# First block of a clustered attention + gated FFN kernel as a software pipeline, with one PSUM tile per logits side

## Chip, cores, metric

One Trainium2 chip, one core of it. The metric is the device time of one execution in microseconds (us), median of several runs. Ratios are computed as the mean time of one kernel's fast runs over the mean of the other kernel's fast runs of the same rounds, so a ratio is not quite the quotient of the medians quoted beside it.

In the text: PE is the matmul engine, DVE the vector engine, ACT the activation engine, POOL the general one. "Issuing queue" is the SyncE queue, from which 146 of the 150 DMAs of the kernel before are issued, in the order of the program. The "granted clock" is the share of full speed at which the profile shows PE's clock: 1.00 is full, 0.50 half. DVE's `avs` step adds the value sums to a finished av result and so frees its bank.

## The reference

Attention in which a key counts for a query only where both fall to the same of 16 clusters, then a gated FFN. Batch 4, 8 heads, sequence 768, head size 64; FFN from 512 to 1536 and back, on 3072 tokens.

```python
q_assign = argmax(einsum('bhsd,hcd->bhsc', q_n, c_n))      # k_assign alike
mask = q_assign[:, :, :, None] == k_assign[:, :, None, :]
scores = where(mask, scale * q @ k.T, -1e9)
attn = softmax(scores); x = attn @ v                       # heads side by side: [3072, 512]
out = (sigmoid(x @ w_gate) * (x @ w_val)) @ w_out
```

## The kernel before

Each batch is done in two blocks (half of the queries each): eight blocks. A block is 24 steps: 4 pairs of heads times 6 chunks of keys. A step makes scores (2 matmuls), one exp on ACT, and, one step later, 6 matmuls with the values ("av"). The FFN of the block before is mixed into it, some 5 matmuls a step; after block 8 its FFN runs alone (the tail).

Before scores can be made, a pair must be prepared: split into high and low halves of fp16 (`hl`), transposed into `T`, multiplied with the centroids (logits), turned into one-hot rows, and these transposed into 16 further rows of `T`. Scores contract over 80 rows of `T`, 64 of data and 16 of one-hot.

```python
    def logits(b, side, pr):                     # one PSUM tile for both sides
        if side == 1:
            CL[b, pr] = fp_.tile([128, 2, 256], FP, name="f")
        ...
    def prep_pe(pr):                             # batch 0, pair by pair, on PE
        for side in (1, 0):
            hl = split(b, side, pr)              # two DVE instructions
            pt = scp.tile([128, 2, 1024], HP, name="sc")
            ... # 12 transposes, copy to T (DVE for side 1, ACT for side 0)
        for side in (1, 0):
            logits(b, side, pr); onehot(...)
        for side in (1, 0):
            ... # 12 transposes of 80 rows, copy of 16 rows into T
    def att(b, qb):                              # 24 steps
        for pr in range(NPR):
            for j in range(NCH):
                ... # scores into sc (2 buffers), exp into es
                yield
                if pend is not None: av_part(*pend)   # at j == 5: avs = av + sv on DVE,
                ...                                   # which frees the only av bank
                yield
    def ffn(b, qb, tail=False):
        for fc in range(NFC):
            for i, w in enumerate((wg, wv)):
                ...
                for dc in range(NDC):
                    nc.tensor.matmul(out=gv[i][:, 0:QB], ...)
                    yield
            g = gp_.tile([128, QB], FP, name="g")
            nc.scalar.activation(g, gv[0][:, 0:QB], AF.Tanh, scale=0.5)
            nc.vector.scalar_tensor_tensor(hT[:, fc, :], g, 1.0, gv[1][:, 0:QB], ALU.add, ALU.mult)
        ...
    def plan(b):                                 # preparation of batch b within batch b-1
        for pr in range(NPR):
            a = 6 + 8 * pr
            at(max(a - 9, 0), load_pair, b, pr)
            at(a, prep_a, b, pr)                 # splits, DMA transpose
            at(a + 8, prep_b, b, 1, pr)          # logits, onehot
            at(a + 9, prep_b, b, 0, pr)
        ...
        at(40, prep_oh, b, 1); at(41, prep_oh, b, 0)   # one-hot: DMA transpose, 8 row DMAs
```

The softmax here doesn't subtract the row's maximum and nothing guards it: scores larger than these inputs give would overflow.

## Time and profile before

| | before |
|---|---|
| time, median of 3 runs | 414.63 us (413.35 to 415.19) |
| span in the profile | 411.4 us |
| first exp starts | 20.99 us |
| block 1, first exp to first exp of block 2 | 58.85 us |
| blocks 2 to 8, same measure (the last to the last exp) | 44.46, 42.42, 45.40, 43.02, 46.65, 38.46, 35.99 us |

Block lengths here and below are counted from the start of every 24th exp in the timeline. Blocks 7 and 8 prepare nothing.

Busy time by stretch, cut where the transpose of a block's output is issued. The columns are stretch, its length, then busy us (and instructions) of PE, weight load, DVE, ACT, POOL, then the granted clock, the DMA share and GB/s:

```profile
core 0: us, PE busy (x) PEld busy (x) DVE busy (x) ACT busy (x) POOL busy (x), PEclk, DMA share, GB/s
0.00:82.50 82.50, 52.88 (x701) 40.93 (x702) 43.95 (x87) 37.18 (x38) 11.56 (x20) 0.75 0.81 199
82.50:126.50 44.00, 39.72 (x414) 24.28 (x413) 16.29 (x36) 26.30 (x37) 6.25 (x8) 0.93 0.25 49
...
303.50:341.20 37.70, 36.02 (x322) 21.41 (x320) 9.41 (x20) 27.17 (x39) 3.29 (x4) 1.00 0.11 33
```

The first stretch leaves PE idle for 30 us at a mean clock of 0.75 (too high: the record of the clock starts at 17.3 us, and what comes before reads as 1.00). The page's line of the clock, in 40 slices of 10.3 us, shows where it was low:

```profile
PEclk9968586569999999999999999989999999999999
```

Part of the chain of waits in the first block (start, us, what). The long step is a DMA transpose for batch 1 that runs while the weights stream in (the last of them, issued at 23.73, landed 31.7 us later); it took 14.7 us to land, where such transposes have a median of 3.5. A load that batch 0 needs stands behind it and the next one on the issuing queue and is issued at 55.72:

```profile
38.03 0.58 DVE avs L309
...
38.82 0.83 DVE T_154 L202
...
41.59 14.72 DMA T_295<-hl
...
56.41 0.57 DVE hl L150
```

Over the whole run the page gives this wait 13.4 us:

```profile
L299 PE MATMUL av<-va,es 128*128 128x65 f16 x1152 | 70.0, 199 | 14.4 <-DVE avs L309 13.4
```

### The profile page before, as it was taken

What the parts mean: (1) busy time and instruction counts of PE and PEld (TensorE: products, weight loads), DVE (VectorE), ACT (ScalarE), POOL (GpSimd) and SP (SyncE); (2) the same over time, 40 slices, a digit from 0 to 9 for tenths busy, and PEclk for the clock granted to TensorE, in tenths of its full rate; (3) what the DMA queues carried; (4) which work ended last, traced back from release to release, by engine and by line L of the source; (5) the groups of instructions that cost most, each with busy time, mean ns of one, the idle gap of its engine ahead of it and who ended that gap; (6) DMA issues with size and microseconds to landing.
All of it is one profiled execution on the core that took longest, in us unless ns stands there. A gap on an engine that the chain in (4) does not pass through costs nothing.

```text
span 411.4 us, 8513 instructions
## 1 busy us (share of the span) xinstructions
PE 355.7 (86%) x3602; PEld 222.2 (54%) x3602; DVE 159.3 (39%) x327; ACT 237.3 (58%) x324; POOL 43.5 (11%) x56
## 2 busy tenths in 40 slices
PE   1675956888899989989998989988999999999996
PEld 1653745555555556556554656555545555555552
DVE  4548445525422464254414365154312320232240
ACT  1354444654666767556666755645757766775331
POOL 2140000130000000300000001200000000001000
PEclk9968586569999999999999999989999999999999
DMA  5589998433116936740129476330230003000301
GB/s 194 204 168 228 242 197 249 111 64 78 21 43 181 258 77 231 167 104 2 35 56 281 130 200 185 117 78 2 57 111 27 0 2 91 28 0 3 115 2 76
DMA packets 75623, 45.42 MB, mean 110 GB/s; under 512 B 56896, under 2 KB 71488, under 8 KB 75584
## 3 DMA queue, kind: packets, MB, share of 16 engines
q1 hardware_dynamic: 72832, 40.12, 35.7%
q0 software_dynamic: 2608, 4.72, 6.4%
q8 instruction: 28, 0.46, 0.5%
q14 instruction: 11, 0.09, 0.1%
q10 hardware_dynamic: 144, 0.03, 0.0%
HBM read 28.34 MB, written 6.29 MB: 84 GB/s over the span
## 4 chain that ended last, share of the span: by engine, by line
PE 57%; DVE 13%; ACT 11%; DMA 10%; issue 6%; SPq 0%; POOL 0%; ACTq 0%; DVEq 0%
PE f L376 18%; PE f L393 13%; PE sc L336 10%; ACT es L344 7%; PE av L299 6%; DMA T_295<-hl 4%; DVE avs L309 3%; PE f L165 3%; DVE hl L150 3%; ACT g L385 3%; DVE hl L151 3%; DMA out_dram<-osb 2%; PE sc L376 2%; PE f L273 2%; PE sc L194 1%
## 5 line engine op out<-in xcount | busy, mean ns | idle before, releaser
L344 ACT ACTIVATE es<-sc,nbias 128x768 f16<-128x768 f32 x192 | 172.3, 900 | 122.1 <-PE sc L336 117.5
L386 DVE SCALAR_TENSOR_TENSOR hT<-g,f 128x384 f16<-128x384 f32 x90 | 49.8, 554 | 135.5 <-ACT g L385 107.8
L376 PE MATMUL f<-xT,wg 128*128 128x384 f16 x360 | 92.7, 329 | 5.2 <-ACT g L385 3.6
L299 PEld LDWEIGHTS <-es 128*128 128x128 f16 x1152 | 62.7, 101 | 56.3 <-issue 26.8
L376 PE MATMUL f<-xT,wv 128*128 128x384 f16 x360 | 87.5, 327 | 3.2 <-ACT g L385 2.0
L299 PE MATMUL av<-va,es 128*128 128x65 f16 x1152 | 70.0, 199 | 14.4 <-DVE avs L309 13.4
L393 PE MATMUL f<-wo,hT 128*128 128x512 f16 x288 | 75.7, 379 | 0.0
L321 POOL TENSOR_TENSOR x<-avs,ri 128x384 f16<-128x384 f32 x32 | 26.4, 824 | 319.7 <-DVE ri L320 250.5
L385 ACT ACTIVATE g<-f 128x384 f32<-128x384 f32 x90 | 43.5, 483 | 3.6 <-PE f L376 3.6
L376 PEld LDWEIGHTS <-wv 128*128 128x128 f16 x384 | 33.2, 97 | 22.4 <-issue 8.3
L376 PEld LDWEIGHTS <-wg 128*128 128x128 f16 x384 | 34.3, 98 | 18.2 <-issue 1.4
L393 PEld LDWEIGHTS <-hT 128*128 128x128 f16 x288 | 25.3, 97 | 20.5 <-issue 0.4
L336 PE MATMUL sc<-T_153,T_154 80*128 80x384 f16 x96 | 30.4, 410 | 5.4 <-ACT T_153 L227 4.3
L151 DVE SCALAR_TENSOR_TENSOR hl<-nat,hl 128x768 f16<-128x768 f32 x32 | 30.7, 958 | 1.1
L176 DVE TENSOR_REDUCE mx<-f 128x12 f32<-128x192 f32 x32 | 11.3, 352 | 48.9 <-PE f L165 48.9
L150 DVE TENSOR_SCALAR hl<-nat 128x768 f16<-128x768 f32 x32 | 18.5, 578 | 17.4 <-DMA nat<-in_k_dram 15.6
L336 PE MATMUL sc<-T_1737,T_1739 80*128 80x384 f16 x96 | 24.0, 330 | 0.2 <-DMA T_1737<-ohT_2879 0.2
L336 PE MATMUL sc<-T_3046,T_3048 80*128 80x384 f16 x96 | 23.5, 325 | 0.2 <-DMA T_3046<-ohT_4188 0.2
L336 PE MATMUL sc<-T_293,T_295 80*128 80x384 f16 x96 | 23.6, 325 | 0.0
L309 DVE TENSOR_TENSOR avs<-av,sv 128x390 f32<-128x390 f32 x32 | 17.9, 559 | 13.9 <-PE av L299 13.9
L402 ACT ACTIVATE osb<-f 128x512 f32<-128x512 f32 x24 | 14.2, 593 | 14.3 <-PE f L393 12.0
L194 PE MATMUL sc<-ident,hl 128*128 128x128 f16 x96 | 10.5, 273 | 12.7 <-DVE hl L151 12.2
(76 smaller groups left out, 211.0 us busy)
## 6 DMA issues: line engine op xcount, KB each, us to landing
nat<-in_k_dram SPq DMA_DIRECT2D x16, 384.0 KB, 4.5
nat<-in_q_dram SPq DMA_DIRECT2D x16, 384.0 KB, 5.6
vn<-in_v_dram SPq DMA_DIRECT2D x4, 1536.0 KB, 7.5
out_dram<-osb SPq DMA_DIRECT2D x24, 256.0 KB, 2.3
wg<-in_moe_w_gate_dram POOLq DMA_DIRECT2D x1, 1536.0 KB, 11.7
wv<-in_moe_w_val_dram POOLq DMA_DIRECT2D x1, 1536.0 KB, 20.2
wo<-in_moe_w_out_dram POOLq DMA_DIRECT2D x1, 1536.0 KB, 31.7
T_295<-ohT_1538 SPq DMA_DIRECT2D x8, 24.0 KB, 1.8
```

What stands on the lines that cost most here:

```text
L150: nc.vector.tensor_scalar(hl[:, :, 0, :], nat, SC, None, ALU.mult)
L151: nc.vector.scalar_tensor_tensor(hl[:, :, 1, :], nat, SC, hl[:, :, 0, :], ALU.mult, ALU.subtract)
L194: nc.tensor.transpose(pt[:, hh, bass.ts(c, 128)], hl[:, hh * NCH + c, :, :].rearrange("p a d -> p (a d)"), ident,)
L299: nc.tensor.matmul(out=av[:, o : o + D + 1], lhsT=es[:, hh, bass.ts(t, 128)], rhs=VA[b][:, 2 * pr + hh, j, :], start=(j == 0 and hh == 0 a ...
L309: nc.vector.tensor_tensor(s, av[:, 0 : 2 * QCH * (D + 1)].rearrange("p (h t d) -> p h t d", h=2, t=QCH), SV[b][:, 2 * pr : 2 * pr + 2, :] ...
L321: nc.gpsimd.tensor_tensor(x[:, :, 2 * pr * D : 2 * (pr + 1) * D].rearrange("p t (h d) -> p h t d", h=2), s[:, :, :, 0:D], ri.unsqueeze(3). ...
L336: nc.tensor.matmul(out=sc[:, hh, 0:QB], lhsT=T[b, 1][0 : D + NCL, h, bass.ts(j, 128)], rhs=T[b, 0][0 : D + NCL, h, bass.ts(qb, QB)], start ...
L344: nc.scalar.activation(es, sc[:, :, 0:QB], AF.Exp, bias=nbias, scale=es_scale)
L376: nc.tensor.matmul(out=gv[i][:, 0:QB], lhsT=w[:, dc, bass.ts(fc, 128)], rhs=xT[:, :, dc, :], start=(dc == 0), stop=(dc == NDC - 1),)
L385: nc.scalar.activation(g, gv[0][:, 0:QB], AF.Tanh, scale=0.5)
L386: nc.vector.scalar_tensor_tensor(hT[:, fc, :], g, 1.0, gv[1][:, 0:QB], ALU.add, ALU.mult)
L393: nc.tensor.matmul(out=o, lhsT=hT[:, fc, bass.ts(t, 128)], rhs=wo[:, fc, :], start=(fc == 0), stop=(fc == NFC - 1),)
```

## The change

The intent is to prepare pair 1 before the loop and pairs 2 and 3 while pairs 0 and 1 are attended, so that no step of the first block waits for a preparation in series. One-hot rows of pairs 1 to 3 go through one set of 6 transposes per pair and small DMAs. With it come other moves: one PSUM tile per logits side; the tanh directly behind the gate product; batch 1's preparation later (so that it leaves the first block), that of batches 2 and 3 earlier; values loaded in two halves; warm-up matmuls at the start; no special tail. The core of the diff (cuts marked):

```diff
-    natp = ctx.enter_context(tc.tile_pool(name="nat", bufs=4))
+    natp = ctx.enter_context(tc.tile_pool(name="nat", bufs=8))
...
+    warm(14)
...
     def logits(b, side, pr):
-        if side == 1:
-            CL[b, pr] = fp_.tile([128, 2, 256], FP, name="f")
-        cl = CL[b, pr]
+        cl = CL[b, pr, side] = fp_.tile([128, 512], FP, name="f")
...
+    def p_split(pr, side):
+        HL[pr, side] = split(0, side, pr, nc.gpsimd if pr else None)   # first half on POOL
+    def p_trans(pr, side): ...      # 12 transposes, copy into T
+    def p_class(pr, side): ...      # logits, onehot
+    def p_rows(pr): ...             # 6 transposes, one copy, 4 row DMAs
...
-    def ffn(b, qb, tail=False):
+    def ffn(b, qb):
...
+                    if i == 0 and dc == NDC - 1:
+                        g = gp_.tile([128, QB], FP, name="g")
+                        nc.scalar.activation(g, gv[0][:, 0:QB], AF.Tanh, scale=0.5)
                     yield
-            g = gp_.tile([128, QB], FP, name="g")
-            nc.scalar.activation(g, gv[0][:, 0:QB], AF.Tanh, scale=0.5)
...
+        if b == 1:
+            a_at = (18, 24, 30, 35)
+            b_at = (26, 32, 38, 42)
+            oh_at = 44
+        else:
+            a_at = (4, 12, 20, 27)
+            b_at = (12, 20, 28, 35)
+            oh_at = 37
...
+    def plan_first():
+        for pr in range(NPR):
+            o = 2 * NCH * pr
+            if pr + 1 < NPR:
+                at(o + 1, p_rows, pr + 1)
+            if pr + 2 < NPR:
+                at(o, p_split, pr + 2, 1)
+                at(o + 2, p_split, pr + 2, 0)
+                at(o + 4, p_trans, pr + 2, 1)
+                at(o + 6, p_trans, pr + 2, 0)
+                at(o + 8, p_class, pr + 2, 1)
+                at(o + 10, p_class, pr + 2, 0)
```

In `plan`, `a_at` are the steps of the splits and DMA transposes of a pair, `b_at` those of its logits, `oh_at` that of the one-hot transposes; 48 steps make a batch.

## The prediction

> **What bounds the kernel now.** The page gives a 411.4 us span. Cut at the xT transposes (timeline of the DMA-issuing queue), two regimes show. From 82.5 us PE is 90-96% busy: seven attention+FFN blocks of 37.7 to 46.4 us and a 31.7 us tail, bound by PE; each block idles PE 1.7 to 4.3 us. The waits view: after 110 us, av matmuls wait 10.7 us in 19 pieces for the DVE step avs. The timeline (0.58 us at 136.9 and 146.1) shows a queue effect: avs stands behind hT, hT waits for the tanh, the tanh stands behind an exp.
> In the first block scores run from 19.1 to 79.5 us: 24 steps of 2.5 us, though one exp is 0.90. Chain of waits: split (0.55+0.96), transposes, copy (0.95 DVE, 1.44 ACT), logits, onehot, transposes, copy, each pair in series, plus a 14.7 us block-2 DMA transpose under the weight load, behind which a nat load sat until 56.4. One-us stretches show granted clock 0.50 for most of 21-28, 38-51, 58-68, 72-89 us. [...] changes lie about 3.4, 6.8, 10.2 us apart.
>
> **What changes.**
> 1. First block: pair 1 is prepared before the loop, pairs 2,3 during pairs 0,1. The prologue summed from traced durations: first scores near 19.5 us, no later than now, as the Exp table load (1.28 us at 19.7) moves away. Some splits go half to POOL (the va cast of twice the size takes 1.47 us; I estimate 0.8). Row transposes fall from 24 to 6 per pair; their 1.43 us ACT copy vanishes for pairs 1-3. Pairs 0,1 cost PE at half clock 6x1.05 + 24x0.107 + 2x0.7 + 0.65 = 11 us, with bubbles 11-12; at full clock about 8.5. Pairs 2,3: 7.2 or 6. With sv 30 to 41 us; I take 37.5. Block ends near 57, not 79.5: -22, on the critical path.
> 2. Batch 1's preparation moves into block 2: two pairs of logits and splits more there: +3. Its one-hot transposes move from step 40 to 44. That queue chain took 13 us (110.6 to 123.6: transpose 3.1, eight row DMAs 5.0, transpose 2.5, first rows). Four steps are 7 us, so batch 1's first scores stall about 5 us, and the clock may drop: +6. Batches 2,3 go at step 37: no stall.
> 3. Tanh right after the gate product, and shorter-held logits tiles: removes most avs and f waits: -1 to -2 in each of seven blocks, -10.
> 4. Tail on three f tiles: PE is gapless there, a bank has about 0.5 us of slack: 0. Warm-up matmuls fill idle PE: 0.
>
> **Sum.** 414.6 - 22 + 3 + 6 - 10 = about 391 us; range 382 to 401. Faster by over 2%: 0.94; within 2%: 0.05; slower: 0.01.
>
> **What would show it.** First xT transpose near 60 us (82.5 now); first exp near 20; pairs 2,3 at 1.0-1.2 us a step; PE waiting several us for a DMA of T<-ohT once, at batch 1's first scores; av waits for avs near 2 us; tail still 31.5.
>
> **What would make it wrong.** The clock at 0.5 (+4) or full (-8) through the first block; row DMAs of pairs 1-3 late under the weight load; weights still loading when the FFN starts; sc buffers held by copies for over 1.5 us; no stall at batch 1 (-6).

No term of the sum rests on it: 414.6 - 22 + 3 + 6 - 10 = about 391 us stands as it was put on record. The half-clock costs of point 1 are spacings in the profile of the kernel before (12 transposes 1.28 us and 24 logits 0.68 us at 44 to 49 us); that the clock may drop at batch 1's stall, within the +6, was my estimate. What that profile shows of the clock is that in the first 90 us it changed at 20.8, 27.6, 37.8, 51.5, 58.3, 68.5, 72.0 and 89.0 us: 6.8, 10.2, 13.7, 6.8, 10.2, 3.4 and 17.1 us apart.

## More of the kernel before

Unless a run is called slow, it is fast.

A pair boundary in block 7, from the timeline (start, us, engine, line, what; in brackets the idle time before it and its releaser):

```profile
311.47 0.90 ACT L344 ACTIVATE es<-sc,nbias 128x768 f16<-128x768 f32 x1
...
311.70 0.34 PE L299 MATMUL av<-va,es 128*128 128x65 f16 x6
...
312.27 0.48 ACT L385 ACTIVATE g<-f 128x384 f32<-128x384 f32 x1
...
312.79 0.56 DVE L386 SCALAR_TENSOR_TENSOR hT<-g,f 128x384 f16<-128x384 f32 x1 [11.33 <-ACT g L385]
...
312.81 0.48 PE L376 MATMUL f<-xT,wv 128*128 128x384 f16 x2
...
313.26 0.56 DVE L309 TENSOR_TENSOR avs<-av,sv 128x390 f32<-128x390 f32 x1
...
313.87 0.34 PE L299 MATMUL av<-va,es 128*128 128x65 f16 x6 [0.58 <-DVE avs L309]
```

The line at 311.70 is the last av group of a pair. The exp holds ACT until 312.37, so the tanh (`g`), queued behind it, comes late; `hT` waits for it; `avs` stands behind `hT` on DVE and starts 1.56 us after the av group; and PE waits for `avs` to free the av bank, until 313.87. DVE did not let `avs` pass here: by its record the av group was over at 312.04, DVE stood idle until 312.79, and yet `avs` started 0.47 us after `hT`.

## The result, and the profile after

| | before | after |
|---|---|---|
| time, median of 4 runs | 414.91 us (413.35 to 416.19) | 382.78 us (379.75 to 386.18) |
| ratio of fast runs | | 0.920 (0.913 to 0.927) |
| span in the profile | 411.4 us | 381.8 us |
| first exp | 20.99 us | 21.54 us |
| block 1 | 58.85 us | 37.58 us |
| block 2 | 44.46 us | 51.89 us |
| blocks 3 to 8 | 42.42, 45.40, 43.02, 46.65, 38.46, 35.99 | 45.05, 39.70, 42.33, 39.71, 35.64, 33.23 |
| blocks 3 to 8 together | 251.9 us | 235.7 us |
| from the start of the last exp to the end | 35.2 us | 35.2 us |

One of the four runs (386.18 us) counts as slow; the fast three average 381.8 us. That is just under the low end of the predicted range, 382; the forecast gain was 23.6 us, and the fast runs gained 33. The two profiled runs (413.2 and 383.7 us) lie 29.5 apart; the rest is spread between runs, so by how much the range was missed is in part chance.

The same view by stretch as before, at the corresponding cuts:

```profile
core 0: us, PE busy (x) PEld busy (x) DVE busy (x) ACT busy (x) POOL busy (x), PEclk, DMA share, GB/s
0.00:60.40 60.40, 49.83 (x569) 31.35 (x570) 33.55 (x65) 32.92 (x36) 25.36 (x26) 0.75 0.91 228
60.40:113.00 52.60, 43.06 (x503) 27.60 (x501) 25.29 (x51) 26.62 (x37) 6.91 (x7) 0.82 0.49 98
...
278.80:314.40 35.60, 35.60 (x325) 21.83 (x324) 9.41 (x20) 27.58 (x40) 3.31 (x4) 1.00 0.12 34
```

The first stretch is 22 us shorter. That the mean clock reads the same says little: here its record starts at 6.9 us, before the change at 17.3. The second is longer. The seventh block's stretch is 2.1 us shorter at these cuts and has no idle PE at all: 35.60 busy of 35.60. Its pair boundary now reads:

```profile
287.28 0.49 ACT L425 ACTIVATE g<-f 128x384 f32<-128x384 f32 x1
...
287.65 0.91 ACT L388 ACTIVATE es<-sc,nbias 128x768 f16<-128x768 f32 x1
287.71 0.34 PE L343 MATMUL av<-va,es 128*128 128x65 f16 x6
287.82 0.56 DVE L427 SCALAR_TENSOR_TENSOR hT<-g,f 128x384 f16<-128x384 f32 x1 [9.98 <-ACT g L425]
...
288.30 0.56 DVE L353 TENSOR_TENSOR avs<-av,sv 128x390 f32<-128x390 f32 x1
...
288.72 0.49 PE L416 MATMUL f<-xT,wv 128*128 128x384 f16 x2
...
289.04 0.34 PE L343 MATMUL av<-va,es 128*128 128x65 f16 x6
```

PE has the same order here as before. The tanh now stands ahead of the exp in ACT's queue; `avs` starts 0.59 us after the last av group (1.56 before) and ends at 288.86, before the two products from 288.72 are through, so PE goes on to the next av group at 289.04 without a wait. On the page the wait is down from 13.4 to 5.5 us, and the clock line is still low in the first third:

```profile
PEclk9859655799959989999999989999999999999999
...
L343 PE MATMUL av<-va,es 128*128 128x65 f16 x1152 | 70.9, 200 | 6.7 <-DVE avs L353 5.5
```

What lengthens block 2 is one wait, at batch 1's first scores; the granted clock went from 1.00 to 0.50 at 105.9 us, within the wait, and back at 116.1, and two score matmuls after the wait take twice as long (0.99 us, against 0.49):

```profile
101.96 0.60 PE L434 MATMUL f<-wo,hT 128*128 128x512 f16 x2
109.92 0.99 PE L380 MATMUL sc<-T_421,T_423 80*128 80x384 f16 x2 [7.36 <-DMA T_421<-ohT_1649]
```

So the sums that the prediction gave for blocks 1 and 2 stand (-20.7 with the later first exp, +7.4), and blocks 3 to 8 gave 16.3 us where I had about 9. The sum, -20.7 + 7.4 - 16.3 = -29.6, is the change of the span.

### The profile page after: what moved, and what is told of

Read it like the earlier page. It is cut to its first block, busy times and chain, and to the rows that moved or that the text cites. A ratio compares the mean times of both kernels' runs of the same rounds, so it can differ in the third digit from the quotient of the medians.

```text
span 381.8 us, 8564 instructions
## 1 busy us (share of the span) xinstructions
PE 352.7 (92%) x3570; PEld 218.5 (57%) x3570; DVE 161.7 (42%) x319; ACT 234.5 (61%) x322; POOL 59.7 (16%) x62
## 4 chain that ended last, share of the span: by engine, by line
PE 80%; DMA 5%; issue 4%; POOL 3%; DVE 3%; ACT 2%; SPq 1%; ACTq 0%; POOLq 0%; DVEq 0%
PE f L416 33%; PE f L434 17%; PE sc L380 16%; PE av L343 9%; PE f L186 3%; DMA nat<-in_q_dram 2%; POOL hl L173 2%; DMA xT<-x 2%; PE f L317 1%; ACT es L388 1%; DVE hl L174 1%; DMA ohT_1649<-oh_422 1%; SPq L76 1%; DVE avs L353 1%; DVE hl L173 1%
## 5 line engine op out<-in xcount | busy, mean ns | idle before, releaser
L427 DVE SCALAR_TENSOR_TENSOR hT<-g,f 128x384 f16<-128x384 f32 x96 | 53.0, 553 | 119.8 <-PE f L416 81.8
L416 PE MATMUL f<-xT,wg 128*128 128x384 f16 x384 | 99.0, 333 | 1.2 <-DMA xT<-x 1.2
L416 PE MATMUL f<-xT,wv 128*128 128x384 f16 x384 | 93.2, 329 | 0.5 <-ACT g L425 0.5
L434 PE MATMUL f<-wo,hT 128*128 128x512 f16 x288 | 78.0, 388 | 0.0
L343 PE MATMUL av<-va,es 128*128 128x65 f16 x1152 | 70.9, 200 | 6.7 <-DVE avs L353 5.5
L365 POOL TENSOR_TENSOR x<-avs,ri 128x384 f16<-128x384 f32 x32 | 27.9, 873 | 285.6 <-DVE ri L364 214.1
L425 ACT ACTIVATE g<-f 128x384 f32<-128x384 f32 x96 | 46.8, 487 | 23.5 <-PE f L416 13.8
L416 PEld LDWEIGHTS <-wg 128*128 128x128 f16 x384 | 34.5, 99 | 19.5 <-issue 3.6
L416 PEld LDWEIGHTS <-wv 128*128 128x128 f16 x384 | 33.5, 98 | 16.3 <-issue 1.5
L174 DVE SCALAR_TENSOR_TENSOR hl<-nat,hl 128x768 f16<-128x768 f32 x32 | 33.5, 1046 | 3.0 <-POOL hl L173 2.1
L380 PE MATMUL sc<-T_184,T_185 80*128 80x384 f16 x96 | 31.4, 420 | 0.5
L380 PE MATMUL sc<-T_421,T_423 80*128 80x384 f16 x96 | 24.7, 337 | 7.4 <-DMA T_421<-ohT_1649 7.4
L353 DVE TENSOR_TENSOR avs<-av,sv 128x390 f32<-128x390 f32 x32 | 17.9, 559 | 20.6 <-PE av L343 20.5
L380 PE MATMUL sc<-T_1731,T_1733 80*128 80x384 f16 x96 | 23.9, 330 | 0.0
L380 PE MATMUL sc<-T_3046,T_3048 80*128 80x384 f16 x96 | 23.5, 325 | 0.0
L380 PEld LDWEIGHTS <-T_423 80*128 80x128 f16 x96 | 9.6, 101 | 15.9 <-issue 9.1
```

Source lines behind the costliest of these rows:

```text
L174: nc.vector.scalar_tensor_tensor(hl[:, :, 1, :], nat, SC, hl[:, :, 0, :], ALU.mult, ALU.subtract)
L343: nc.tensor.matmul(out=av[:, o : o + D + 1], lhsT=es[:, hh, bass.ts(t, 128)], rhs=VA[b][:, 2 * pr + hh, j, :], start=(j == 0 and hh == 0 a ...
L353: nc.vector.tensor_tensor(s, av[:, 0 : 2 * QCH * (D + 1)].rearrange("p (h t d) -> p h t d", h=2, t=QCH), SV[b][:, 2 * pr : 2 * pr + 2, :] ...
L365: nc.gpsimd.tensor_tensor(x[:, :, 2 * pr * D : 2 * (pr + 1) * D].rearrange("p t (h d) -> p h t d", h=2), s[:, :, :, 0:D], ri.unsqueeze(3). ...
L380: nc.tensor.matmul(out=sc[:, hh, 0:QB], lhsT=T[b, 1][0 : D + NCL, h, bass.ts(j, 128)], rhs=T[b, 0][0 : D + NCL, h, bass.ts(qb, QB)], start ...
L416: nc.tensor.matmul(out=gv[i][:, 0:QB], lhsT=w[:, dc, bass.ts(fc, 128)], rhs=xT[:, :, dc, :], start=(dc == 0), stop=(dc == NDC - 1),)
```

## The experiments

Every kernel below gave a correct result and was timed in 3 rounds beside the kernel before (4 runs each with the profiled one). "Blocks 3-8" is the sum of those six lengths in the profile. Block lengths are of one execution each. Blocks 7 and 8 repeat to 0.02 us, but block 1 took 35.3 to 38.9 us in kernels whose first block has the same code (the changed one, tanh late, the old steps with and without the moved value sum, splits at 10), so a difference of 2 or 3 us in block 1 alone shows nothing.

| kernel | time, median | ratio to before | block 1 | block 2 | blocks 3-8 |
|---|---|---|---|---|---|
| before | 414.6 | 1 | 58.9 | 44.5 | 251.9 |
| after | 382.8 | 0.920 | 37.6 | 51.9 | 235.7 |
| before, tanh early | 403.7 | 0.975 | 58.5 | 44.0 | 239.3 |
| before, new steps | 410.6 | 0.994 | 58.0 | 45.3 | 247.2 |
| before, tanh early and new steps | 399.5 | 0.966 | 59.3 | 43.6 | 234.1 |
| before, logits tiles | 411.9 | 0.996 | 57.9 | 44.4 | 251.5 |
| before, batch 1 late | 416.4 | 1.007 | 53.2 | 54.3 | 250.8 |
| after, tanh late | 399.2 | 0.964 | 37.0 | 53.3 | 249.8 |
| after, shared logits tile | 383.5 | 0.926 | 36.6 | 51.5 | 236.9 |
| after, old steps | 396.6 | 0.956 | 38.3 | 51.4 | 246.8 |
| after, old steps, shared tile | 393.2 | 0.949 | 39.7 | 51.9 | 243.2 |
| after, old steps, value sums at 34 | 389.8 | 0.942 | 38.9 | 51.3 | 243.0 |
| after, batch 1 four steps earlier | 373.7 | 0.906 | 37.3 | 43.3 | 232.8 |
| after, scores over 128 rows | 376.2 | 0.910 | 34.5 | 48.8 | 233.0 |
| after, no warm-up | 381.4 | 0.920 | | | |
| after, splits at 10 | 381.4 | 0.922 | 35.3 | 50.9 | 235.9 |

### Which part did I undersize?

The rivals: the tanh order, the logits tiles, or the new steps.

Tanh put back in the changed kernel:

```diff
-                    if i == 0 and dc == NDC - 1:
-                        g = gp_.tile([128, QB], FP, name="g")
-                        nc.scalar.activation(g, gv[0][:, 0:QB], AF.Tanh, scale=0.5)
                     yield
+            g = gp_.tile([128, QB], FP, name="g")
+            nc.scalar.activation(g, gv[0][:, 0:QB], AF.Tanh, scale=0.5)
```

> The changed kernel with the tanh put back behind the value product. Blocks are counted by exps (24 each); in the changed kernel blocks 3 to 8 together take 235.7 us, 16.3 less than before. Theory T (the tanh order is what I undersized): blocks 4, 6, 7, 8 come back to within 1 us of before's (45.4, 46.7, 38.5, 36.0), total about 396 to 398 us. Theory L (the logits tile is it): blocks 4 and 6 stay near 40 to 41, only blocks 7, 8 and a little elsewhere move; total about 386 to 388. Theory S (the moved steps): the same as L for blocks 4 and 6, blocks 7 and 8 near 38.

399.22 us, ratio 0.964 (0.961 to 0.967). Blocks 7 and 8 came back to 38.47 and 35.98, before's lengths to 0.02 us. Blocks 4 and 6 rose by 3.0 and 2.7 only, to 42.7 and 42.5, not to before's 45.4 and 46.7. So the tanh is the main part, and something else works in blocks 4 and 6.

One logits tile again in the changed kernel (`CL[b, pr]`, allocated for side 1 and used by both):

> The changed kernel with one PSUM tile for the logits of both sides again. Theory T: blocks 4 and 6 rise by at most 1 us each, total within 2 us of 382. Theory L: blocks 4 and 6 rise by 3 to 5 us each, total 388 to 392. Blocks 7 and 8 have no logits and must stay at 35.6 and 33.2 in every theory.

383.54 us, ratio 0.926; blocks 4 and 6 unchanged (39.70, 39.71). The tiles are not it.

The old steps for batches 2 and 3 in the changed kernel:

```diff
-            a_at = (4, 12, 20, 27)
-            b_at = (12, 20, 28, 35)
-            oh_at = 37
+            a_at = (6, 14, 22, 30)
+            b_at = (14, 22, 30, 38)
+            oh_at = 40
```

> The changed kernel with the old steps for batches 2 and 3 (splits at 6, 14, 22, 30; logits at 14, 22, 30, 38; one-hot transposes at 40). Theory S (logits at step 30 meet a pair boundary): blocks 4 and 6 rise by 3 us or more each, total near 389. Theories T and L: blocks 4 and 6 stay within 1 us. The splits at step 4 stall blocks 3 and 5 by 2.3 us (an av matmul waits for avs behind a split that waits for its load); if so, step 6 shortens blocks 3 and 5 by 1.5 to 2.5 us each, total near 378.

396.64 us, ratio 0.956: the steps do matter, and more than any theory said. Blocks 4 and 6 rose by 8 us each (47.65, 48.12); blocks 3 and 5 fell to 41.1 and 39.5.

The tanh alone moved in the kernel before:

> The kernel before with only the tanh moved to right behind the gate product. Theory T: blocks 4, 6, 7, 8 fall to about 41, 41, 35.7, 33.3, blocks 2, 3, 5 by 1.5 to 2 each; total near 399. Theory L: blocks 7 and 8 fall by 2.8 each, blocks 4 and 6 by at most 2; total near 406. My prediction's sizing (10 us in seven blocks for tanh and tiles together) would give 405 or more.

403.71 us, ratio 0.975 (0.973 to 0.978). Blocks 3 to 8 fell by 12.6 us; block 8 by 2.8, block 7 by 1.1; blocks 4 and 6 to 43.3 and 46.6, above what theory T asked. The mechanism was mine, the size was not: this one line is worth more than I gave to tanh and tiles together.

The total would have fallen further, but the tail grew from 35.2 to 39.5 us. In this kernel the tail still puts the gate and the value product of every second `fc` into one PSUM tile (`both`), and now the value product waits there for the tanh that reads the gate half, six times:

```profile
371.59 0.81 PE L376 MATMUL sc<-xT,wg 128*128 128x384 f16 x4
372.98 0.81 PE L376 MATMUL sc<-xT,wv 128*128 128x384 f16 x4 [0.58 <-ACT g L385]
```

Where nothing waits, a group of four starts 0.65 us after the one before; here it is 1.39. Six times 0.74 us is 4.4, the growth of the tail. The changed kernel has the early tanh without this, as it dropped the special tail: 35.2.

### Do tanh and steps depend on each other?

> The kernel before with the tanh early and batches 2 and 3 on the new steps (splits 4, 12, 20, 27; logits 12, 20, 28, 35; one-hot transposes 37); nothing else. With the tanh alone, blocks 3 to 7 took 206.1 us in sum; in the changed kernel 202.4. Theory I (the two are complementary: quicker steps leave the old chain of fixed DMA latencies too little time, the new steps give it back): blocks 3 to 7 near 203, blocks 4 and 6 at 40 to 41, total near 400. Rival O (the rest of the change, the logits tile and the halved value loads, makes up the difference): blocks 4 and 6 stay above 43, total near 404.

399.48 us, ratio 0.966. Blocks 4 to 8 are 39.70, 42.54, 39.70, 35.65, 33.22, within 0.2 us of the changed kernel's 39.70, 42.33, 39.71, 35.64, 33.23. So tanh and steps are all that shortened blocks 4 to 8; value halves, tiles and the rest give nothing there. (The tail is 39.5 us here too.) I took this for theory I. The last corner of the square is the steps alone:

> The kernel before with batches 2 and 3 on the new steps and the tanh left late: the last corner of the square of tanh and steps (neither 414.6, tanh 403.7, both 399.5). Complementary (theory I): the steps alone give 0 to 3 us, total 411 to 414, blocks 3 to 6 together 1 to 3 us below before's 177.5. If tanh and steps simply add, the steps alone give 4 us and the total is 410.

410.55 us, ratio 0.994 (0.989 to 0.999). Blocks 3 to 8: neither 251.9, tanh 239.3 (-12.6), steps 247.2 (-4.8), both 234.1 (-17.8). The two add to -17.4, so theory I falls as it was written: the steps alone give more than it allowed. But they do not simply add. Block by block, both together give 5.2 us more than the sum of the two in blocks 4, 6 and 7 (block 6: tanh -0.1, steps -4.2, both -6.9), and 4.8 us less in blocks 3 and 5; that the total adds is a cancellation. The traces show what theory I had in mind. The DMA chain of a batch's one-hot rows, from its first transpose to the end of its last row DMA on the issuing queue, took 15.7, 16.0 and 15.6 us in the kernel before (16.1, 16.3 and 15.7 in the changed one), and over these blocks PE waits 0.4 us for batches 2 and 3's one-hot rows (`T<-ohT`) in the kernel before, 3.4 us with the tanh alone, and not at all with both. Against it stand two waits of 2.3 us for `avs` in blocks 3 and 5, which appear with both (below; with the steps alone the longest is 0.7). The steps, which I had written down as 0, are worth 4.8 us by this sum; the ratio of the timed runs gives 2.6 (0.5 to 4.7).

### The logits tiles alone

> The kernel before with one PSUM tile per logits side and nothing else. From the after side (shared tile: blocks 3 to 8 together 236.9 against 235.7) the tiles are worth about 1 us: total 412 to 415, blocks 7 and 8 unchanged. My prediction had counted 3 to 4 us on them: total near 411.

411.85 us, ratio 0.996 (0.992 to 0.999). Blocks 3 to 8 changed by 0.5 us; the rest stands in block 1 (57.9 against 58.9), within its spread. Together with the shared tile above the tiles are worth about 1 us in blocks 3 to 8.

### Why are the old steps so bad in the changed kernel?

They have the same steps as the kernel before with the early tanh, but blocks 3 to 8 take 246.8 us against 239.3.

> The changed kernel with the old steps for batches 2 and 3 and the shared logits tile. The old steps alone gave blocks 3 to 7 of 41.1, 47.7, 39.5, 48.1, 37.2. If the separate tiles ask for banks at the wrong moment there (logits wait 2.4 us for an eviction in block 4), blocks 4 and 6 fall to 43 to 46 and the total to about 389 to 391. If not, blocks 4 and 6 stay within 1 us and the total near 396.

393.21 us. Blocks 4 and 6 fell by 1.2 and 0.9 us, and block 7 by 1.5: less than expected of the tiles.

> The changed kernel with the old steps for batches 2 and 3 and both value sums at step 34, so that none stands at step 40 beside the one-hot transposes. If that meeting is the cause, blocks 4 and 6 fall by 2 us or more each; if not, they stay within 1 us of 47.7 and 48.1.

(The edit moves the second value sum from step 40 to 34.) 389.79 us. Blocks 4 and 6 fell by 1.3 and 1.5: neither of the two answers expected. Each edit takes away about half of the difference (3.6 and 3.8 of 7.5 us in blocks 3 to 8), also in block 7, which both bring back to 35.65. Whether the two halves add was not run; this stays open. Nor was it run whether the value halves or the earlier loads (10 steps ahead, 9 before) play a part. The waits of PE in these blocks say where the time goes: 4.8 us for one-hot rows and 4.7 us of logits for the output copy `osb`; with the shared tile 4.3 and 2.8, with the moved value sum 2.9 and 3.7.

### What the steps do

The timeline of the changed kernel in block 5: both splits of step 12 stand on DVE just ahead of a pair boundary, which is every sixth step.

```profile
214.91 0.55 DVE L173 TENSOR_SCALAR hl<-nat 128x768 f16<-128x768 f32 x1
...
215.49 0.96 DVE L174 SCALAR_TENSOR_TENSOR hl<-nat,hl 128x768 f16<-128x768 f32 x1
...
216.37 0.55 DVE L173 TENSOR_SCALAR hl<-nat 128x768 f16<-128x768 f32 x1
...
216.96 0.96 DVE L174 SCALAR_TENSOR_TENSOR hl<-nat,hl 128x768 f16<-128x768 f32 x1
217.83 0.55 DVE L427 SCALAR_TENSOR_TENSOR hT<-g,f 128x384 f16<-128x384 f32 x1
218.30 0.56 DVE L353 TENSOR_TENSOR avs<-av,sv 128x390 f32<-128x390 f32 x1
218.89 0.19 DVE L364 RECIPROCAL ri<-avs 128x6 f32<-128x6 f32 x1
218.90 0.49 PE L343 MATMUL av<-va,es 128*128 128x65 f16 x6 [2.27 <-DVE avs L353]
```

The old steps had a split at 30, also a pair boundary, in the second block of the batch; there `avs` waits reach 1.0 us before the change. So the move took a boundary split out of blocks 4 and 6 and put one into blocks 3 and 5. To test it, the split of step 12 went to step 10:

> The changed kernel with only the second pair's splits of batches 2 and 3 at step 10 and not 12 (a pair boundary). If splits on a pair boundary cost the 2.3 us waits of av for avs, both waits vanish, blocks 3 and 5 fall by 2 to 3 us each (from 45.1 and 42.3), blocks 4 and 6 stay at 39.7, total near 377. If the waits come from something else, blocks 3 and 5 stay within 1 us and the total near 382.

381.40 us, ratio 0.922, the same as the changed kernel. Both waits of av for `avs` vanished, as the first theory said, but blocks 3 and 5 stayed (44.99, 42.62). In their place stands a wait of PE for the output copy on ACT (`osb`), which waits for an earlier store to land. SPq is the issuing queue:

```profile
194.37 0.59 ACT L443 ACTIVATE osb<-f 128x512 f32<-128x512 f32 x1
...
196.04 0.85 SPq L76 DMA_DIRECT2D nat<-in_k_dram  x1
...
197.99 0.47 SPq L76 DMA_DIRECT2D nat<-in_q_dram  x1
198.56 0.89 SPq L444 DMA_DIRECT2D out_dram<-osb  x2
...
204.98 0.60 ACT L443 ACTIVATE osb<-f 128x512 f32<-128x512 f32 x1 [2.30 <-DMA out_dram<-osb]
205.63 0.38 PE L416 MATMUL f<-xT,wg 128*128 128x384 f16 x1 [2.14 <-ACT osb L443]
```

The copy of 194.37 was ready at 194.96, but its store was issued only at 198.56, behind four loads, and landed some 6 us later. My edit did this: a pair's load goes ten steps ahead of its split, so the second pair's load moved from step 2 to step 0, ahead of the stores. The wait behind splits on a boundary is thus shown, but what its removal is worth is not: a wait of nearly equal length (2.14 against 2.27 us), made by the same edit, took its place. How the 4.8 us of the steps divide between boundaries and the rest stays open.

### Block 1: the pipeline, or batch 1 out of the way?

The kernel before with batch 1's preparation at the late steps (18 to 45):

> The kernel before with only batch 1's preparation moved to the late steps of the change (18 to 45). It tells how much of the first block's 21 us comes from the freedom from batch 1's work and its DMA transpose under the weight load, and how much from the pipeline of preparation. If the collision is a large part: block 1 falls from 58.9 to 52 or less. If the series of each pair's preparation is what counts: block 1 stays at 55 or more. Block 2 should rise by 6 to 9 in both cases, with one wait of 4 us or more for the row DMAs at batch 1's first scores; total 412 to 420.

416.41 us, ratio 1.007. Block 1 fell from 58.9 to 53.2, in between the two answers; block 2 rose by 9.8, more than expected, with a wait of 6.0 us for the row DMAs. Of block 1's 21.3 us, 5.7 is batch 1 leaving it; the other 15.6 is put down to the pipeline by subtraction, as no kernel had the pipeline alone. The 5.7 us are more than paid back in block 2.

### The wait at batch 1

The changed kernel with batch 1 four steps earlier:

```diff
-            a_at = (18, 24, 30, 35)
-            b_at = (26, 32, 38, 42)
-            oh_at = 44
+            a_at = (14, 20, 26, 31)
+            b_at = (22, 28, 34, 38)
+            oh_at = 40
```

> The changed kernel with batch 1's preparation four steps earlier (splits 14, 20, 26, 31; logits 22, 28, 34, 38; one-hot transposes 40). The 7.4 us wait for the row DMAs at batch 1's first scores should fall to under 1 us and block 2 from 51.9 to about 45; block 1 may lengthen by 1 to 3 us, as one more split, a transpose and logits land in it. Total 376 to 379. If block 2 stays above 50 the wait was not the cause of its length.

373.65 us, ratio 0.906 (0.900 to 0.912), better than expected. The wait fell from 7.4 to 2.1 us, block 2 from 51.9 to 43.3, block 3 from 45.1 to 42.2, and block 1 did not lengthen (37.3). The late steps were put there to free block 1, and cost 6 us by the two ratios to the kernel before (9 by the medians) for nothing. Block 2 has one pair more of splits and logits here than before the change, and yet is no longer than with the early tanh alone (44.0).

### The clock

In the profiled run of the changed kernel PE is 90 to 97% busy between 40 and 60 us (by its records, which run on past the start of the next matmul: 0.33 us for 384 columns, where starts lie 0.163 us apart at full clock) and yet at about half clock (0.55 and 0.50 below). Scores contract over 80 of 128 rows there. Rows 80 to 127 of `T` hold low halves, whose products are below the result's precision, so the same number of columns can be run over all rows:

```diff
-                        lhsT=T[b, 1][0 : D + NCL, h, bass.ts(j, 128)],
-                        rhs=T[b, 0][0 : D + NCL, h, bass.ts(qb, QB)],
+                        lhsT=T[b, 1][:, h, bass.ts(j, 128)],
+                        rhs=T[b, 0][:, h, bass.ts(qb, QB)],
```

> The changed kernel with the scores contracted over all 128 rows of T and not 80 (the other 48 rows hold low parts, whose products are far below the result's precision; same column count). If the clock's grant depends on how many rows are busy, the mean clock of the first 60 us rises from 0.75 to 0.85 or more and block 1 falls by 3 us or more. If it depends on time or columns only, the clock and block 1 (37 to 38 us) stay, total within 2 us of 382.

376.17 us, ratio 0.910 (0.907 to 0.913). First the changed kernel, then this one, then the changed kernel with its splits at 10 (a run from above, with 80 rows and the same first block), same view as before (the clock is the third column from the right):

```profile
40.00:50.00 10.00, 9.71 (x118) 5.81 (x114) 6.36 (x12) 7.65 (x8) 1.63 (x1) 0.55 0.57 182
50.00:60.00 10.00, 9.01 (x65) 3.97 (x64) 2.20 (x6) 7.19 (x9) 1.47 (x2) 0.50 0.88 233
```

```profile
40.00:50.00 10.00, 8.83 (x136) 5.85 (x135) 6.36 (x12) 7.85 (x9) 1.63 (x1) 0.83 0.66 200
50.00:60.00 10.00, 6.64 (x97) 3.69 (x98) 3.36 (x7) 7.57 (x10) 2.63 (x4) 1.00 0.91 236
```

```profile
40.00:50.00 10.00, 8.17 (x137) 5.22 (x136) 6.26 (x12) 8.21 (x9) 1.63 (x1) 1.00 0.61 190
50.00:60.00 10.00, 7.94 (x67) 3.90 (x67) 3.30 (x6) 6.98 (x8) 2.57 (x4) 0.61 0.89 236
```

Block 1 fell by 3.1 us, block 2 by the same, and the result is still correct. The third pair of lines warns against reading the first two as proof: with 80 rows too this stretch can have full clock for 10 us, and block 1 took 35.3 us there. The better evidence is the mean clock of the timed runs: 0.924 to 0.937 in the three fast ones of the changed kernel, 0.952 to 0.964 in these four; and 0.940 to 0.946 against 0.964 to 0.970 with batch 1 early (best1 below has the 128 rows). So more rows on the same columns went with a higher clock. That it is the count of rows, and not something else that came with the edit, such as the values in them, was not separated.

### No warm-up

The three `warm` calls taken out of the changed kernel:

> The changed kernel without the 14 + 4 + 4 warm-up matmuls. The prediction gave them 0. If they matter, the first transposes run at half clock, the first exp comes later than 21.5 us by 1 us or more and the total is above 384. If not: first exp at 20.5 to 21.6, total within 2 us of 382.

381.43 us, ratio 0.920. The 0 stands. The profiled run was a slow one (384.78 us), so its blocks are left out of the table; its first exp, before any of that matters, is at 21.58 us (21.54 with it). The matmuls did shorten early work: the first 12 transposes of a side take 1.46 us without them and 0.84 with them. That the clock does this is my reading; without them the view reads 1.00 over the first 20 us, and so does not show it. The first exp came no earlier for it.

### Putting it together

128 rows and the earlier batch 1; then the first split at step 6; then the splits on DVE (`split(0, side, pr)` without the POOL argument); then the splits at step 10 (and 4 again):

> The changed kernel with the scores contracted over 128 rows and batch 1's preparation four steps earlier together. Alone they gave 376.2 and 373.7. If they add: 367 to 369, block 1 near 34.5, block 2 at 41 to 43, block 3 near 41 as no cold stretch follows the stall.

> best1 with the first split of batches 2 and 3 at step 6 and not 4. In the changed kernel blocks 3 and 5 hold one 2.3 us wait of an av matmul for avs, behind a split on the same engine that waits for its load. If so, blocks 3 and 5 fall from about 42.4 to near 40 each and the total is 4 to 5 us under best1; if the wait moves elsewhere, within 1 us of best1.

> best2 with the first half of every split of the first block on DVE (0.55 us) and not on POOL (2.1 us each in the changed kernel, where PE waits 2.4 us at 39 us behind one). If POOL's splits pace the first pairs, block 1 falls by 1 to 3 us; if DVE becomes the limit, it stays or rises by up to 2.

> best3 with step 10 in place of 12 (and step 4 in place of 6). best3 was 372.5 with blocks 3 and 5 of 42.4 and 42.5. If the boundary is the cause, both near 40 and the total 367 to 369; if not, 372.

| kernel | time, median | ratio to before | block 1 | block 2 | blocks 3-8 |
|---|---|---|---|---|---|
| best1 | 373.15 | 0.905 (0.899 to 0.911) | 36.2 | 44.9 | 232.9 |
| best2 | 375.72 | 0.909 (0.902 to 0.915) | 34.8 | 46.6 | 233.9 |
| best3 | 372.47 | 0.900 (0.896 to 0.904) | 34.5 | 47.4 | 232.8 |
| best4 | 370.78 | 0.900 (0.893 to 0.907) | 36.7 | 42.0 | 232.3 |

Most of these expectations missed. The two gains do not add: with batch 1 early, the 128 rows give back in block 2 what they gain in block 1 (blocks 1 and 2 together are 80.6 us with the earlier batch 1 alone and 81.1 with both). Step 6 does nothing, as the wait was at step 12. Splits on DVE leave block 1 as it was (34.8 to 34.5), so POOL's do not pace it there. The fastest is best4 at 370.78 us, 10% under the kernel before and 2 to 3% under the change (2.2% by the ratios, 3.1% by the medians); its interval overlaps those of the other three, so which of them is best is not settled. In best3's block 2 the waits that end last are 3.2 us for the transposed output and 2.8 us for batch 1's rows, both from the issuing queue.

## Why the prediction was right or wrong, point by point

- **First block, "-22": right.** First exp +0.55 us, block 1 -21.3 us: -20.7. The length of 37.5 us was met (37.58), with the clock at half for some 24 us of it (mean 0.68), the case that I had between my two sums. The first exp "near 20" came 1.5 us late. My estimate for a POOL split, 0.8 us, was far off (2.17 us); with 128 rows, splits on DVE changed block 1 by 0.3 us only.
- **Block 2, "+3" and "+6": right in the sum, the parts not shown.** With the tanh late, as the sum counted it, block 2 is 53.3 against 44.5: +8.9. The wait was 7.4 us and not "about 5"; the "several us for a DMA of T<-ohT once" appeared as written, and half clock came with it, from 105.9 to 116.1 us. A longer wait than the one summed leaves less room for the "+3" of more work, of which no run shows anything; that the sum was met is in part luck. That the move need not have cost this was not seen.
- **"Tanh right after the gate product, and shorter-held logits tiles: removes most avs and f waits: -1 to -2 in each of seven blocks, -10": this is the step that failed, in its size.** The queue effect was as described. But the tanh alone is worth 13.1 us in blocks 2 to 8 of the kernel before (0.5 + 12.6) and 15.6 us in the changed one (block 2 1.5, blocks 3 to 8 14.1), the tiles about 1. I took the waits that the profile reports as the most there was to gain. They are not all. In the stretch of block 7 the profile reports three waits of PE, 0.58 + 0.58 + 0.41 = 1.57 us, and 1.68 us of idle PE. Counting from the start of each group of matmuls in the timeline to the start of the next, less the group's matmuls at the spacing that they have where nothing waits (0.163 us for 384 columns, 0.031 for an av matmul), 2.84 us are lost, at nine places; in the changed kernel's block 7 none. The block became 2.82 us shorter. Two parts were hidden. Each reported wait is about 0.16 us too short: after the two products at 312.81 the next could have started at 313.14, it started at 313.87, and 0.58 is reported. And six waits of 0.1 to 0.3 us are not in the list of waits: five end within the record of the matmul before, and of the sixth (0.27 us) 0.11 shows as idle time. The records show why: that of a matmul of 384 columns is 0.32 to 0.33 us long where the next starts 0.163 us after it, so it runs on by 0.16 us over whatever follows. So 1.57 us are reported and 2.84 us lost. The same holds beyond block 7: with the tanh alone moved, the idle time of PE in blocks 3 to 8 fell by 8.0 us (17.9 to 9.9), the blocks by 12.6.
- **"Batches 2,3 go at step 37: no stall": a second, smaller miss.** No stall for rows came, but the new steps brought two waits of 2.3 us for `avs`, and I gave them no value, while they are worth 4.8 us in blocks 3 to 8 of the kernel before.
- **Tail and warm-up, 0 each: right, but the tail only as a whole.** 35.2 us from the last exp to the end in both kernels; the slack that I had estimated at 0.5 us is there (in the changed kernel the bank of the tail's first value product is free at 356.46 and written again at 356.93 us); without warm-up the ratio is 0.920 as well. With the tanh early, the old tail costs 4.4 us, so leaving it out is part of what the tanh gains. I counted the two moves apart.
- **Signs given beforehand.** First output transpose near 60: at 60.43. Pairs 2 and 3 at 1.0 to 1.2 us a step: 7.2 and 7.9 us for six, so 1.2 and 1.3. Av waits near 2 us: no, 5.5, of which two of 2.3 are the new ones behind step 12's splits.

## What to carry to other kernels

Size a PE stall from start to start of the matmuls, not from the idle time that the profile reports: where records run 0.16 us over the next start, as here, the short waits vanish and the long ones shrink, here to 55% of the loss (1.57 of 2.84 us). Put an instruction into its engine's queue when its input is ready, not where the code that uses it stands: one line moved was worth 10 us alone, after 4.4 us that it cost in the tail, where both halves shared a tile. And when work is moved out of the way of one stage, count the DMA chain that follows it (here 15.6 to 16.3 us, six times in two kernels) at its new place against the steps left there; in the kernel before it cost 9.8 us in block 2 and freed 5.7 in block 1.

## What else the traces showed

- Matmuls can keep PE busy without full clock: 90 to 97% busy by its records at a clock of 0.50 to 0.55 between 40 and 60 us with scores over 80 rows (another run with 80 rows had 1.00, then 0.61 there). The mean clock of a fast run was 0.924 to 0.937 with 80 rows and 0.952 to 0.964 with 128.
- A scaling of 128x768 from fp32 to fp16 took 2.17 us on POOL and 0.55 us on DVE, though a plain cast of twice the size took 1.49 us on POOL:

```profile
L173 POOL TENSOR_SCALAR hl<-nat 128x768 f16<-128x768 f32 x6 | 12.9, 2172 | 4.1 <-DMA nat<-in_k_dram 4.1
L310 POOL CAST va<-vn 128x1536 f16<-128x1536 f32 x2 | 3.0, 1493 | 0.0
```

- The clock record of a trace can start late: in the kernel before it reads 1.00 over the first 20 us (its first entry is at 17.3 us), while 12 transposes take 1.46 us at 7.2 us; at 19.5 us, in the same trace, 12 of the same take 0.83 us.
